# State weights turned on the matrix engine instead of the vector engine, and a shifted weight conversion, in an attention block that feeds a gated MLP

## The chip, the cores and the metric

The kernel runs on one core of a Trainium2 chip. A core has a matrix engine (TensorE, PE in the profile; its weight loads are PEld), a vector engine (VectorE, DVE), a scalar engine (ScalarE, ACT), GpSimd (POOL) and a sync engine (SP) that here only issues transfers. The engines run their own instruction streams in order and wait for each other by semaphores. The metric is device time in microseconds (us) of one execution; lower is better.

## The reference

Two blocks follow each other. The first is attention between 512 tokens and 32 state rows per head, in both directions; the second is an MLP over the 8 x (512 + 32) = 4352 rows that the first one makes, with the gate h·cos(h).

```python
B, H, S, Ns, D = 8, 8, 512, 32, 64           # d_model 512, d_ff 2048
scores  = x @ state.T / sqrt(D);  a  = softmax(scores);   xread = a @ state
scores2 = state @ x.T / sqrt(D);  a2 = softmax(scores2);  sread = a2 @ x
x2 = concat([xread, sread], axis=2)          # to (B*(S+Ns), H*D)
h = x2 @ w_in
out = (h * cos(h)) @ w_out
```

The weights arrive as 64-bit floats and are turned into 32-bit floats on the chip.

## The kernel before, in words

The order of all work is written out by hand. The loop at the end of the kernel goes through 144 tiles ("steps"): 16 for the tokens of each of the 8 batches (one tile is 128 of the 2048 hidden columns, for 512 tokens), and 16 for the state rows of all batches together. This text calls the 16 steps of batch b "loop b" and numbers them 0 to 15.

What one step does, in the order in which it is issued: `hidden` (L479) makes h in a PSUM bank, out of `aT` (the normalised attention weights of the batch) and `sw` (the product of state and w_in, so that xread is never formed); there are two such banks, so the h of a step waits for the last reader of h two steps before. `gate` (L485, ACT) rounds, `gate2` (L488, DVE) subtracts, `gate3` (L493, L494, ACT) takes Abs and Sin, `gate4` (L500, DVE) multiplies h by the cosine and writes the tile g. `output` (L544) multiplies g of the tile three steps back (four in loop 0) with w_out.

The output product takes pairs of batches and computes 7 block products instead of 8, in the manner of Strassen and Winograd: w_out lies in four blocks a11, a12, a21, a22; `blocks` (L858, POOL) makes the sums s1, s2, s4 and s3 of them once, s3 in the place of a21; `minus` (L506) makes differences of g. The two halves of the loops are phases: 0 and 1 in even loops, 2 and 3 in odd ones. Products that a pair leaves over (`p7` with s3, `p4` with a22) are done during the next pair, one in two of three steps, which is why steps differ in length. `keep_product` (L555 on ACT, L557 on DVE) and `plus` (L550) take finished products out of PSUM into `held`, `store` (L571) turns them on DVE and SP writes them out.

`plan(b)` says what else is issued at which step of loop b; this is the attention of batch b+1. `pe` is issued right after h, `x_act` and `x_dve` after gate2, `y_act` and `y_dve` after gate4:

- `tokens_turned` (L298, DVE): x of the batch, which SP loaded into `xT`, is transposed in 32x32 blocks. In batches 0 and 1 PE does it (L271) instead.
- `scores` (L316, PE) into the two PSUM banks `at`; `max1` (L330), `spread1` (L336), `shift` (L353), `max2` (L346), `exps` (L357 and L362, ACT, each between loads of the function table), `sums` (L330 again), `norm1` (L383), which leaves `aT`.
- The weights of the state's read, `z2` (in xT[:, 2:4]), have to be transposed into `a2T` (in xT[:, 0:2], where `spread` was). For batches 0 and 1 `turn` (L389) does it with 8 PE transposes and `turn_kept` (L394) copies the results from the banks `at` on ACT. For batches 2 to 7 `turn_block` (L404) does it in 16 DVE transposes of 32x256 elements.
- `reads` (L416, PE), in two halves; after the second one SP is given the loads of the next x (`load_tokens`, 16 transfers into xT, and `load_x`, 4 into x_b). `keep` (L426, DVE), `keep2` (L432, PE) and `keep3` (L437, ACT) finish the state's rows.
- `products` (L316, PE) make `sw` for 512 hidden columns, `products_kept` (L453, ACT) copies it out of PSUM; a quarter serves four steps.

The weight conversion is a chain of parts, `convert`: SP loads 1 MB of raw weights into unused g tiles, ACT makes two passes (parts 1 and 2; L224, L227), DVE three (a, b, c; L231, L233, L236), POOL adds (d; L241), and part f fetches the load three further on. `conv_at` gives the step of parts 1 and 2; the others follow one step later. All of it is in loop 0, with two more at the very end. Conversions 10 and 11 are the last of w_in, 12 and 13 are a12, 14 and 16 a22, 15 and 17 a21.

Of the kernel before, what the change touches and what calls it, by code (L numbers as in the profile page):

```python
# [12 lines left out]
ALU = mybir.AluOpType  # L13
# [10 lines left out]
def kernel(  # L24
# [8 lines left out]
    nc = tc.nc  # L33

    B, H, S, D = x.shape
    Ns = state.shape[2]
    Dm, Dff = moe_w_in.shape
    P = 128
    NK = Dm // P
# [32 lines left out]
    a11, a12 = w_out[:, 0, 0:NH], w_out[:, 0, NH:NF]  # L72
    a21, a22 = w_out[:, 1, 0:NH], w_out[:, 1, NH:NF]
# [174 lines left out]
    class Attention:  # L248
# [147 lines left out]

        def turn_block(self, k, q):
            src = self.z2.rearrange("p j (c q i) -> p q (j c) i", q=P // 32,  # L400
                                    i=32)
            dst = self.a2T.rearrange("p j c m -> p (j c) m")
            rows = slice(Ns * k, Ns * k + Ns)
            nc.vector.transpose(out=dst[32 * q:32 * q + 32, :, rows],  # L404
                                in_=src[rows, q])

        def reads(self, j):  # L410
            cols = slice(2 * D * j, 2 * D * j + 2 * D)
# [49 lines left out]
    def part(b, name, *args):  # L461

        if b not in attn:
            attn[b] = Attention(b)
        getattr(attn[b], name)(*args)
        if (name, args) == ("reads", (1,)) and b + 1 < B:
            if b > 0:
                attn[b + 1] = Attention(b + 1)
                attn[b + 1].load_tokens()
            load_x(b + 1)  # L470
# [21 lines left out]
    def gate3(t):  # L492
        nc.scalar.activation(t.q, t.q, func=ACTF.Abs)  # L493
        nc.scalar.activation(t.q, t.q, func=ACTF.Sin, bias=halfpi,  # L494
                             scale=-TWO_PI)
# [261 lines left out]
    def plan(b):  # L757
        pe, x_act, y_act, x_dve, y_dve = [
            {s: [] for s in range(NF)} for _ in range(5)]

        def prod(s, b, nt, *bank):
            pe[s].append((b, "products", nt) + bank)
            if b == 1 and nt > 0:
                x_dve[s].append((b, "products_taken", nt) + bank)
            else:
                x_act[s].append((b, "products_kept", nt) + bank)

        def pairs(s, b, name, kept, i):
            pe[s] += [(b, name, i), (b, name, i + 1)]
            x_act[s].append((b, kept, i))  # L770
            y_act[s].append((b, kept, i + 1))

        def early(b, s):
            if b == 1:
                pairs(s[0], b, "tokens", "tokens_kept", 0)
                pairs(s[1], b, "tokens", "tokens_kept", 2)
            else:
                for k in range(NK):
                    to = (x_dve, y_dve)[k % 2]
                    to[s[k // 2]].append((b, "tokens_turned", k))  # L780
            pe[s[2]].append((b, "scores"))
            x_dve[s[2]].append((b, "max1"))
            x_dve[s[3]].append((b, "spread1"))
            y_dve[s[3]].append((b, "shift"))
            x_dve[s[4]].append((b, "max2"))
            y_act[s[4]].append((b, "exps"))
            x_dve[s[5]].append((b, "sums"))
            y_dve[s[5]].append((b, "spread1"))
            x_dve[s[6]].append((b, "norm1"))

        def late(b, s):
            if b < 2:
                pairs(s[0], b, "turn", "turn_kept", 0)
            if s[1] is not None:
                pe[s[1]].append((b, "reads", 0))
            pe[s[2]].append((b, "reads", 1))
            x_dve[s[2]].append((b, "keep"))
            if len(s) > 3:
                turned(b, s[3])

        def blocks_turned(b, to):

            for i in range(16):
                to[i * 5 // 16].append((b, "turn_block", i % NK, i // NK))

        def turned(b, s):
            pe[s].append((b, "keep2"))
            x_act[s].append((b, "keep3"))


        if b == 0:
            pe[0].append((0, "products", 0, SIDE, HC, WC))
            y_dve[0] += [(0, "products_taken", 0, SIDE, HC, WC),
                         (0, "inverse2")]
            prod(7, 0, 2, SIDE)
            prod(11, 0, 3)
            prod(13, 1, 0, MAIN)
            late(0, (1, 2, 3, 4))
            early(1, (5, 6, 7, 8, 9, 10, 11))
            late(1, (12, 13, 14))  # L820
        else:


            odd = b % 2
            bank = (SIDE,) if b == 1 else ()
            if b == 1:
                turned(1, 0)
                prod(0, b, 1, MAIN)
            elif odd:
                prod(0, b, 1)  # L830
                turned(b, 1)
            else:
                late(b, (None, None, 0))
                prod(2, b, 1)
                turned(b, 3)
            prod(4, b, 2, *bank)
            prod(9 if odd else 10, b, 3, *bank)
            if b + 1 < B and odd:
                prod(13, b + 1, 0)
                early(b + 1, (2, 3, 5, 6, 7, 8, 9))  # L840
                blocks_turned(b + 1, (x_dve[12], y_dve[12], x_dve[13],
                                      y_dve[13], x_dve[14]))
                pe[15].append((b + 1, "reads", 0))
            elif b + 1 < B:
                early(b + 1, (4, 5, 6, 7, 8, 9, 10))
                blocks_turned(b + 1, (y_dve[10], x_dve[11], y_dve[11],
                                      x_dve[12], y_dve[12]))
                late(b + 1, (None, 13, 14))
                prod(15, b + 1, 0)
        return pe, x_act, y_act, x_dve, y_dve  # L850


    conv_at = {s: 4 + i for i, s in enumerate(
        (0, 1, 2, 3, 4, 5, 6, 7, 8, 10, 11, 12, 13, 14))}
    conv_at.update({B * NF + 5: N_LOADS, B * NF + 7: N_LOADS + 1})

    def blocks(op, out_, a, b, r):
        nc.gpsimd.tensor_tensor(out_[:, r], a[:, r], b[:, r], op=op)  # L858

    lo, hi = slice(0, NH // 2), slice(NH // 2, NH)  # L860
    block_at = {15: (ALU.add, s1, a21, a22, lo),
                17: (ALU.add, s1, a21, a22, hi),
                18: (ALU.subtract, s2, s1, a11, lo),
                19: (ALU.subtract, s2, s1, a11, hi),
                20: (ALU.subtract, s4, a12, s2, lo),
                21: (ALU.subtract, s4, a12, s2, hi),
                22: (ALU.subtract, s3, a11, a21, lo),
                23: (ALU.subtract, s3, a11, a21, hi)}
    LAG = 3

    line = []
# [1 line left out]
    for step, t in enumerate(all_tiles):  # L873
        s = step % NF
        if s == 0 and t.b < B:
            steps = plan(t.b)
        todo = [p[s] if t.b < B else [] for p in steps]

        def go(n):
            for p in todo[n]:  # L880
                part(*p)

        last, conv = conv_at.get(step - 1, -1), conv_at.get(step, -1)
        if step == B * NF + (0 if f64 else 8):
            fetch(N_LOADS + 2)
        if step == 4:
            warm(1, acc[MAIN][0])
        if step != 1:
            hidden(t)
        if step == 0:  # L890
            hidden(all_tiles[1])
            warm(3, acc[MAIN][0])
            gate(t)
            gate2(t)
            convert(3, "bcdf")
            convert(4, "1a")
            go(0)
        else:
            go(0)
            if step == 5:  # L900
                states(1, acc[SIDE][1])
            gate(t)
            gate2(t)
            if step == 3:
                warm(4, acc[MAIN][0])
                part(0, "products", 1, SIDE)
                part(0, "products_kept", 1, SIDE)
            go(1)
            go(3)
            if step == 1:  # L910
                convert(4, "bcdf")
            elif last >= 0:
                convert(last, "abcdf")
            if conv >= 0 and not todo[1]:
                convert(conv, "1")
        gate3(t)
        if later:
            later.pop(0)()
        gate4(t)
        if conv >= 0 and todo[1] and step > 0:  # L920
            convert(conv, "1")
        if t.pair is not None:
            sums(t)
        if step == 6:
            states_kept(1, acc[SIDE][1])
        go(2)
        if conv >= 0:
            convert(conv, "2")
        go(4)
        if step in block_at:  # L930
            blocks(*block_at[step])
        if t.pair is not None:
            sums2(t)
        while len(line) >= (LAG if step >= 2 * NH else LAG + 1):
            output(line.pop(0))
        line.append(t)
# [32 lines left out]
```

## Time and profile before

| | |
|---|---|
| median of 5 runs | 795.44 us (794.85 to 795.65) |
| profiled execution: time, span | 795.71 us, 793.9 us |
| granted PE clock | 0.997 of full speed |
| busy: PE, DVE, ACT, POOL | 766.5, 472.9, 383.0, 178.5 us |
| DVE: L404, 32x256 transposes | 96, 41.8 us |
| ACT: L394, copies of turned weights | 4, 2.3 us |
| POOL: L858, block sums | 8, 18.8 us |

Busy time counts instructions in flight; a matrix instruction's end is modelled, so that consecutive ones overlap by some tenths of a microsecond. The distance between starts tells more. In timeline lines the columns are start and length in us, engine, source line, operation, tiles (written <- read), array use, shape and number of instructions merged into the line; a bracket holds the engine's idle time just before and what ended it. In lines of waits they are who waited for whom, total us, number of times and the longest.

### The profile page before, as it was taken

Reading aid. Unit: us, or ns where it says so; the run is one execution under the profiler, and the core shown is the slowest. Engines: PE = TensorE matmul, PEld = TensorE weight load, DVE = VectorE, ACT = ScalarE, POOL = GpSimd, SP = SyncE. Lnnn points to the kernel's source line nnn. Section 1 sums busy time; section 2 is a strip of 40 time slices with the busy share of each in tenths; the row PEclk is TensorE's granted clock in tenths of the full one; section 3 lists DMA queues with packets and bytes.
Section 4 is the critical chain, followed back from the end, with each engine's and each line's share of the span. In section 5 each row is a group of like instructions: output and inputs, shape, how many; then the busy total and the mean of one; then the engine's idle time right before and its main releaser. Section 6 shows DMA issues by size and latency. Waiting matters only on the chain.

```text
span 793.9 us, 7552 instructions
## 1 busy us (share of the span) xinstructions
PE 766.5 (97%) x2616; PEld 336.9 (42%) x2616; DVE 472.9 (60%) x771; ACT 383.0 (48%) x614; POOL 178.5 (22%) x119
## 2 busy tenths in 40 slices
PE   8998899899999999999999999999999999999997
PEld 4443333344443444344344444344444444455554
DVE  5879887762468567773658467853566456432531
ACT  3877964642445445643464436433463445322222
POOL 2343358683000000451000000740000004610200
PEclk9999999999999999999999999999999999999999
DMA  8585371003210520105000710105100114000021
GB/s 238 159 229 195 114 152 28 0 1 61 45 26 1 97 49 14 27 4 103 14 13 5 129 27 3 25 14 93 27 0 1 26 28 101 31 1 13 14 40 40
DMA packets 161957, 43.48 MB, mean 55 GB/s; under 512 B 153920, under 2 KB 153920, under 8 KB 161920
## 3 DMA queue, kind: packets, MB, share of 16 engines
q1 hardware_dynamic: 161024, 42.49, 24.6%
q10 hardware_dynamic: 768, 0.39, 0.2%
q8 instruction: 20, 0.33, 0.2%
q0 software_dynamic: 128, 0.13, 0.1%
q14 instruction: 17, 0.14, 0.1%
HBM read 34.08 MB, written 8.91 MB: 54 GB/s over the span
## 4 chain that ended last, share of the span: by engine, by line
PE 69%; DVE 13%; ACT 13%; issue 2%; DMA 1%; POOL 1%; SPq 0%; DVEq 0%; POOLq 0%
PE o L544 37%; PE h L479 22%; PE at L316 4%; PE o L664 3%; DVE q L488 3%; ACT q L493 3%; ACT q L494 3%; DVE g_all L500 2%; DVE xT L404 2%; PE at L416 2%; ACT xT L362 1%; ACT q L485 1%; DVE xT L336 1%; ACT L494 1%; ACT aT L357 1%
## 5 line engine op out<-in xcount | busy, mean ns | idle before, releaser
L479 PE MATMUL h<-aT,sw 128*128 128x512 f32 x512 | 241.6, 594 | 15.0 <-DVE g_all L500 12.8
L544 PE MATMUL o<-g_all,w_out 128*128 128x512 f32 x512 | 236.9, 599 | 1.2 <-POOL w_out L241 1.2
L506 POOL TENSOR_TENSOR g_all<-g_all 128x512 f32<-128x512 f32 x80 | 112.0, 1420 | 454.3 <-DVE g_all L500 450.8
L485 ACT ACTIVATE q<-h 128x512 f32<-128x512 f32 (+1 forms) x144 | 82.1, 570 | 258.9 <-PE h L479 258.9
L488 DVE SCALAR_TENSOR_TENSOR q<-q,h 128x512 f32<-128x512 f32 (+1 forms) x144 | 94.1, 654 | 188.7 <-ACT q L485 188.2
L544 PE MATMUL o<-g_all,s 128*128 128x512 f32 x384 | 177.8, 598 | 0.5 <-DVE held L557 0.5
L500 DVE TENSOR_TENSOR g_all<-h,q 128x512 f32<-128x512 f32 (+1 forms) x144 | 94.9, 659 | 103.0 <-ACT q L494 99.4
L479 PEld LDWEIGHTS h<-aT,sw 128*128 128x128 f32 x512 | 96.3, 190 | 139.9 <-issue 111.6
L544 PEld LDWEIGHTS o<-g_all,w_out 128*128 128x128 f32 x512 | 93.9, 190 | 127.0 <-issue 120.4
L493 ACT ACTIVATE q<-q 128x512 f32<-128x512 f32 (+1 forms) x144 | 87.6, 609 | 110.9 <-DVE q L488 110.8
L544 PEld LDWEIGHTS o<-g_all,s 128*128 128x128 f32 x384 | 71.1, 190 | 94.9 <-issue 87.9
L494 ACT ACTIVATE q<-q,halfpi 128x512 f32<-128x512 f32 (+1 forms) x144 | 100.5, 698 | 4.5
L404 DVE STREAM_TRANSPOSE xT<-xT 32x256 f32<-32x256 f32 x96 | 41.8, 435 | 1.8
L241 POOL TENSOR_TENSOR w_out<-w_out,s 128x1024 int32<-128x1024 int32 x10 | 23.9, 2392 | 79.4 <-DVE w_out L236 79.4
L506 DVE TENSOR_TENSOR g_all<-g_all 128x512 f32<-128x512 f32 x48 | 33.2, 692 | 1.6
L453 ACT COPY sw<-at 128x512 f32<-128x512 f32 x50 | 26.8, 588 | 9.0 <-PE at L316 9.0
L479 PE MATMUL h<-sT,w_in 128*128 128x256 f32 x128 | 30.2, 379 | 0.0
L664 PE MATMUL o<-w_out,g_all 128*128 128x512 f32 x64 | 29.6, 592 | 0.0
L479 PEld LDWEIGHTS h<-sT,w_in 128*128 128x128 f32 x128 | 24.3, 190 | 10.1 <-issue 6.2
L316 PE MATMUL at<-w_in,stT 64*32 64x512 f32 x400 | 27.2, 601 | 0.0
L241 POOL TENSOR_TENSOR w_in<-w_in,s 128x1024 int32<-128x1024 int32 (+1 forms) x10 | 19.6, 1964 | 32.7 <-DVE w_in L236 18.6
L550 DVE SCALAR_TENSOR_TENSOR held<-o,held 128x512 f32<-128x512 f32 x40 | 25.4, 680 | 2.4 <-PE o L544 2.3
(84 smaller groups left out, 453.9 us busy)
## 6 DMA issues: line engine op xcount, KB each, us to landing
out_dram<-ot SPq DMA_DIRECT2D x132, 64.0 KB, 2.0
g_all<-in_moe_w_out_dram SPq DMA_DIRECT2D x8, 1024.0 KB, 5.2
g_all<-in_moe_w_in_dram SPq DMA_DIRECT2D x6, 1024.0 KB, 5.2
xT<-in_x_dram SPq DMA_DIRECT2D x96, 64.0 KB, 2.4
x_b<-in_x_dram SPq DMA_DIRECT2D x24, 256.0 KB, 4.7
x_b<-in_x_dram SPq DMA_DIRECT2D x16, 128.0 KB, 4.2
g_all<-in_moe_w_in_dram SPq DMA_DIRECT2D x4, 512.0 KB, 6.1
x_b<-in_moe_w_out_dram SPq DMA_DIRECT2D x1, 1024.0 KB, 6.2
```

Of the source, the lines that this page charges most:

```text
L241: nc.gpsimd.tensor_tensor(bits, bits, e.bitcast(I32), op=ALU.add)
L316: nc.tensor.matmul(out=(to or at)[j][Ns * k:Ns * k + Ns, 0:n], lhsT=w[D * j:D * j + D, self.b, Ns * k:Ns * k + Ns], rhs=r(slice(D * j, D * ...
L404: nc.vector.transpose(out=dst[32 * q:32 * q + 32, :, rows], in_=src[rows, q])
L479: nc.tensor.matmul(out=t.hp, lhsT=t.lhs(i), rhs=t.rhs(i), start=(i == 0), stop=(i == t.kn - 1))
L485: nc.scalar.activation(t.q, t.hp, func=ACTF.Copy, bias=MAGIC)
L488: nc.vector.scalar_tensor_tensor(out=t.q, in0=t.q, scalar=MAGIC, in1=t.hp, op0=ALU.subtract, op1=ALU.subtract)
L493: nc.scalar.activation(t.q, t.q, func=ACTF.Abs)
L494: nc.scalar.activation(t.q, t.q, func=ACTF.Sin, bias=halfpi, scale=-TWO_PI)
L500: nc.vector.tensor_tensor(t.g, t.hp, t.q, op=ALU.mult)
L506: engine.tensor_tensor(out, a, b, op=ALU.subtract)
L544: nc.tensor.matmul(out=acc[bank][ch], lhsT=w[:, i, P * ch:P * ch + P], rhs=g.g, start=(i == 0), stop=(i == NH - 1))
L664: nc.tensor.matmul(out=acc[MAIN][i], lhsT=t.g[:, P * i:P * i + P], rhs=w_out[:, :, t.f, :], start=(t.n_th == 0), stop=(t.n_th == NF - 1))
```

## The change

`turn_block` and its scheduling go; every batch uses `turn` on PE and `turn_kept` on ACT. Even and odd loops now have one plan: products at steps 0, 4, 9 and 14, token transposes at steps 1 and 2 (loop 1: 2 and 3, as before), scores at 5, exps at 7, norm1 at 9, turns at 10, reads at 11 and 12, keep2 at 15. Before, even loops had their products at steps 2, 4, 10 and 15, the token transposes at 4 and 5, scores at 6, exps at 8, norm1 at 10 and reads at 13 and 14, and the second reads of odd loops stood at step 0 of the following one.

In loop 0, conversions 10 to 17 are issued one step later than before (steps 6 and 9 of loop 0 now start none, before it was 9 alone), so the last ends in loop 1. The block sums s1, s2, s4 follow one step later, and s3 is made in loop 2 (steps 32 and 33 of the whole sequence) and not in loop 1 (22 and 23). In step 3 the copies of a product out of PSUM are issued after Abs and Sin of that step, not before them.

```diff
-        def turn_block(self, k, q):
-            src = self.z2.rearrange("p j (c q i) -> p q (j c) i", q=P // 32,
-                                    i=32)
-            dst = self.a2T.rearrange("p j c m -> p (j c) m")
-            rows = slice(Ns * k, Ns * k + Ns)
-            nc.vector.transpose(out=dst[32 * q:32 * q + 32, :, rows],
-                                in_=src[rows, q])
...
         def late(b, s):
-            if b < 2:
-                pairs(s[0], b, "turn", "turn_kept", 0)
-            if s[1] is not None:
-                pe[s[1]].append((b, "reads", 0))
+            pairs(s[0], b, "turn", "turn_kept", 0)
+            pe[s[1]].append((b, "reads", 0))
             pe[s[2]].append((b, "reads", 1))
...
         else:
-            odd = b % 2
             bank = (SIDE,) if b == 1 else ()
             if b == 1:
                 turned(1, 0)
-                prod(0, b, 1, MAIN)
-            elif odd:
-                prod(0, b, 1)
-                turned(b, 1)
-            else:
-                late(b, (None, None, 0))
-                prod(2, b, 1)
-                turned(b, 3)
+            prod(0, b, 1, *[MAIN for _ in bank])
             prod(4, b, 2, *bank)
-            prod(9 if odd else 10, b, 3, *bank)
-            if b + 1 < B and odd:
-                prod(13, b + 1, 0)
-                early(b + 1, (2, 3, 5, 6, 7, 8, 9))
-                blocks_turned(b + 1, (x_dve[12], y_dve[12], x_dve[13],
-                                      y_dve[13], x_dve[14]))
-                pe[15].append((b + 1, "reads", 0))
-            elif b + 1 < B:
-                early(b + 1, (4, 5, 6, 7, 8, 9, 10))
-                blocks_turned(b + 1, (y_dve[10], x_dve[11], y_dve[11],
-                                      x_dve[12], y_dve[12]))
-                late(b + 1, (None, 13, 14))
-                prod(15, b + 1, 0)
+            prod(9, b, 3, *bank)
+            if b + 1 < B:
+                prod(14, b + 1, 0)
+                early(b + 1, (1 + (b == 1), 2 + (b == 1), 5, 6, 7, 8, 9))
+                late(b + 1, (10, 11, 12, 15))
...
     conv_at = {s: 4 + i for i, s in enumerate(
-        (0, 1, 2, 3, 4, 5, 6, 7, 8, 10, 11, 12, 13, 14))}
+        (0, 1, 2, 3, 4, 5, 7, 8, 10, 11, 12, 13, 14, 15))}
...
-    block_at = {15: (ALU.add, s1, a21, a22, lo),
-                17: (ALU.add, s1, a21, a22, hi),
-                18: (ALU.subtract, s2, s1, a11, lo),
-                19: (ALU.subtract, s2, s1, a11, hi),
-                20: (ALU.subtract, s4, a12, s2, lo),
-                21: (ALU.subtract, s4, a12, s2, hi),
-                22: (ALU.subtract, s3, a11, a21, lo),
-                23: (ALU.subtract, s3, a11, a21, hi)}
+    block_at = {16: (ALU.add, s1, a21, a22, lo),
+                18: (ALU.add, s1, a21, a22, hi),
+                19: (ALU.subtract, s2, s1, a11, lo),
+                20: (ALU.subtract, s2, s1, a11, hi),
+                21: (ALU.subtract, s4, a12, s2, lo),
+                22: (ALU.subtract, s4, a12, s2, hi),
+                32: (ALU.subtract, s3, a11, a21, lo),
+                33: (ALU.subtract, s3, a11, a21, hi)}
...
                 part(0, "products", 1, SIDE)
-                part(0, "products_kept", 1, SIDE)
             go(1)
...
         gate3(t)
+        if step == 3:
+            part(0, "products_kept", 1, SIDE)
         if later:
```

More of the change, by code (lines that the diff above doesn't have):

```diff
@@ L799, in late @@
                 turned(b, s[3])
-        def blocks_turned(b, to):
-            for i in range(16):
-                to[i * 5 // 16].append((b, "turn_block", i % NK, i // NK))
         def turned(b, s):
```

## The prediction

> **What bounds the kernel now.** I read the page's engine shares first, then the matrix engine's (PE's) waits, then PE's timeline tile by tile. A *step* is one tile: PE's group at L479, named h, followed by what is issued until the next h. "Loop b" is the 16 steps 0 to 15 of batch b; its loop also prepares batch b+1.
>
> ```profile
> PE 766.5 (97%) x2616; PEld 336.9 (42%) x2616; DVE 472.9 (60%) x771; ACT 383.0 (48%) x614; POOL 178.5 (22%) x119
> ```
>
> PE is the bound: 27 us of 793.9 are not busy, so an engine taken off the vector engine (DVE) gains only where PE waits for it.
>
> ```profile
> PE h L479 <- DVE g_all L500: 12.8, 9, 2.7
> PE h L479 <- ACT sw L453: 2.2, 2, 1.7
> PE at L416 <- DVE xT L404: 0.6, 3, 0.2
> PE o L544 <- DVE held L557: 0.5, 2, 0.2
> ```
>
> Of the 12.8 us, 3.1 lie after 160 us; most waits are in loop 0, where weights are converted, and in loop 1. But a modelled matmul end hides part of a wait, so I go by start times. A quad (four 128x512 matmuls) takes 1.72 us from start to start (387.31 to 389.03 below), a 16-matmul group at L316 or L416 1.22 with its change-over (6.37 us for a step that holds one and three quads, 5.15 without). Any surplus is a stall. Loop 4 (even), PE:
>
> ```profile
> 387.31 1.88 PE L479 MATMUL h<-aT,sw 128*128 128x512 f32 x4
> 389.03 1.88 PE L544 MATMUL o<-g_all,w_out 128*128 128x512 f32 x4
> 390.75 1.88 PE L479 MATMUL h<-aT,sw 128*128 128x512 f32 x4
> 392.56 2.00 PE L316 MATMUL at<-xT,stT 64*32 64x512 f32 x16
> 394.48 1.98 PE L544 MATMUL o<-g_all,w_out 128*128 128x512 f32 x4
> ...
> 430.39 0.43 PE L416 MATMUL at<-x_b,xT 128*64 128x128 f32 x2
> 431.01 1.09 PE L416 MATMUL at<-x_b,xT 128*64 128x128 f32 x14 [0.19 <-DVE xT L404]
> ```
>
> The scores at 392.56 start on three quarters of their input: the last token transpose (L298) runs on DVE from 392.67. Step 6 takes 7.27 us where 6.37 is its work: 0.90 lost. Step 13 takes 5.28 against 4.65: 0.63 lost to the last L404. Step 11 takes 5.31 against 5.15: 0.17. Loops 2 and 6 show the same to 0.02. Loop 3 (odd), PE:
>
> ```profile
> 325.55 1.88 PE L544 MATMUL o<-g_all,s 128*128 128x512 f32 x4
> 329.00 1.98 PE L479 MATMUL h<-aT,sw 128*128 128x512 f32 x4 [1.57 <-DVE g_all L500]
> 330.82 2.74 PE L544 MATMUL o<-g_all,s 128*128 128x512 f32 x6
> 333.79 1.13 PE L544 MATMUL o<-g_all,s 128*128 128x512 f32 x2 [0.23 <-DVE held L557]
> ```
>
> Step 10 is 5.17 us for two quads (3.43): 1.74 lost, behind exps (step 7), sums and norm1 on DVE. Step 11 is 5.75 for 5.15: 0.60 lost at L557. Loop 5 repeats it; loop 1 loses 2.13 and 0.10 there.
>
> **The change part by part.** The profiled execution took 795.71 us around its span of 793.9, 0.27 above the median of 795.44; I take the same difference off the median.
>
> *Turns on PE.* Removed: 96 DVE transposes at L404, 0.436 us each, 41.8 us in six batches. Added: 8 PE transposes per batch and two ScalarE (ACT) copies of 0.574 (L394). Their price is in loop 0, which does them already:
>
> ```profile
> 51.19 1.04 PE L271 MATMUL at<-ident,x_b 128*128 128x128 f32 x8
> 52.06 0.60 PE L142 MATMUL o<-ident,s 128*128 128x128 f32 x4
> ...
> 89.64 1.04 PE L389 MATMUL at<-ident,xT 128*128 128x128 f32 x8
> 90.51 1.88 PE L544 MATMUL o<-g_all,w_out 128*128 128x512 f32 x4
> ```
>
> Eight take 0.87 us start to start, both times. In loops 2, 4, 6 step 10 has no stall: 3 x 0.87 = +2.6. In loops 1, 3, 5 they fall between 325.55 and 329.00, into the 1.74 (or 2.13) stall: 0, or +2.6 if that cover goes. The copies: the first waits for norm1 (it overwrites `spread`), which ends at 327.7, and fits into ACT's idle 2.37 us before 330.30; the second delays ACT's L555 from 331.60 to 332.2, before PE needs that bank (332.5). Behind it, the next L485 slips 0.5, and DVE's L488 at 333.66 hides that: 0. Bounds 0 to 12 x 0.574 = +6.9, taken 0 because ACT is idle by 1 to 3 us in these steps.
>
> [...]
>
> *Even loops, stalls removed.* The token transposes move to steps 1 and 2, the scores to step 5: 0.90 goes. No L404 holds the reads or L557: 0.63 and 0.17 go. 3 x 1.70 = -5.1. Next late would be what stalls odd loops: exps now in step 7, norm1 in 9. Here PE reaches the h of step 11 by two quads and the turns later (1.72 + 1.72 + 0.87 = 4.3), DVE has three L506 of 0.69 less; 4.3 + 2.1 - 1.74 leaves 4.7 us of slack. Bounds: -5.1 to 0.
>
> *Odd loops.* The first reads now stand in step 11 between h and the quads that wait for L557; their 1.22, moved from step 15, cover the 0.60: -1.2 in loops 3 and 5, -0.1 in loop 1. Bounds -1.3 to 0. The stall of step 10 stays: its chain is the same.
>
> *Other moves.* Second reads with keep (DVE, 4 x 0.295) go to step 12, where DVE has lost 2.7 us of L404; keep2 and keep3 to step 15; products from 2, 10, 13 or 15 to 0, 9, 14: same instructions, same PE time, 0. With the second reads go 16 xT and 4 x_b loads on SP: they block it 12.4 us for xT (from 432.13) and land 2.4 later, about 3 steps; they are needed 5 steps on (about 26 us). Stores queue behind them as now; the next, three steps later, waits at most 1 to 2 us, for nobody. 0; if a load came late, one step of 5 us.
>
> *Loop 0.* PE, DVE and ACT take turns here. (a) Step 3: the two sw copies wait for PE until 43.64, with Abs and Sin behind them; now these run in ACT's 3.08 us of idleness before. The product on DVE (47.07, after 1.99 idle) can follow at 45.1. PE gains nothing until step 5 (it waits for POOL's w_out until 47.65); from then ACT is about 1.4 ahead and PE's 0.51 wait at 57.05 goes. (b) Step 7 loses its conversion (0.65 + 0.69 + 1.22 on DVE). DVE's L488 of step 8, at 69.64, now follows h, two conversion parts and ACT's L485: 67.9, 1.74 earlier. (c) Steps 8 to 11 hold as many conversions as before; the chain of waits is ACT and DVE throughout, so 1.74 remains. (d) The conversion at step 11, though, is now the first half of a12, which before was done at step 9:
>
> ```profile
> 90.74 1.22 DVE L236 SCALAR_TENSOR_TENSOR w_out<-g_all,w_out 128x1024 int32<-128x1024 int32 x1
> ...
> 92.11 2.36 POOL L241 TENSOR_TENSOR w_out<-w_out,s 128x1024 int32<-128x1024 int32 x1 [9.05 <-DVE w_out L236]
> ```
>
> POOL's add ends at 94.47 - 1.74 = 92.7; the first product with a12 (step 12, 90.51 before) would be ready at 88.8 and waits 3.9 us. From there PE's own work to the h of loop 1 is 1.82 + 14.03 (92.62 to 106.65, unstalled): 108.6, against 108.41, whose 1.76 stall is used up. +0.2. Lower end -0.5 (DVE's product, 107.9, then bounds); upper end +1.9 (no 1.74). (e) The last conversion is now in step 16, ahead of that step's product: it ends at 117.9, and h needs it at 118.6. POOL's first half of s1 ends at 123.2, needed at 123.8. 0; one more POOL op of 2.37 if not.
>
> *s3.* Two POOL ops of 2.36 leave steps 22 and 23, where nobody waited, for 32 and 33; p7 reads them three steps later. 0.
>
> **Sum:** +2.6 - 5.1 - 1.3 + 0.2 = -3.6, so 795.44 - 3.6 = 791.8 us.
>
> **Rivals.** (A) The late a12 keeps PE waiting and no head start reaches it: +1.7 on the sum, 793.5. For: two handovers between ACT and DVE decide it. Against: freed DVE time is in the rows. (B) The turns show in odd loops too, because the stall shrinks with DVE's relief: +2.6, 794.4. Against: no L404 stood before step 10. (C) Slower than before: exps one step earlier in even loops, ahead of the short step 8, put the odd loops' stall there. Each pays 1.74 + 0.60, hiding its 0.87: 3 x 1.47 = +4.4 on the sum, 796.2, and past 797.0 from another 0.3 us a loop. It decides once more than the 4.7 us of slack is used. Against: nothing in the rows uses it. (D) Better: the a12 wait is shorter and DVE bounds, or odd stalls shrink with turns hidden: -4.3 to -5.5, 791 to 790.
>
> **How the numbers follow.** Forecast 0.53, A 0.15, B 0.10, C 0.12, D 0.10. Own range of the forecast 790.9 to 792.8. The range 790.3 to 794.6 leaves out C and part of D. 0.2% (1.6 us) is about what a measurement can tell: faster, below 793.85, holds the forecast, D and two thirds of A, 0.73; same the rest of A, B and a third of C, 0.19; slower, above 797.03, two thirds of C, 0.08.
>
> **What would show it.** Right: steps 6 and 13 of even loops free of surplus, step 10 of 6.0 us there; step 10 of odd loops unchanged near 5.2 with eight transposes in it; a POOL wait of 3 to 4 us before step 12's product in loop 0, and loop 1's first h near 108.6. Wrong: a DVE wait at h in even loops, h of loop 1 past 110, or PE waiting for xT loads at the scores.

## The result, and the profile after

| | before | after |
|---|---|---|
| median | 795.42 us (43 executions) | 793.92 us (23 executions), 0.9981 of before, 95% interval 0.9975 to 0.9986 |
| profiled execution: time, span | 795.71, 793.9 | 793.92, 792.1 |
| granted PE clock, mean | 0.997 | 0.994 |
| busy: PE, DVE, ACT | 766.5, 472.9, 383.0 | 769.8, 430.3, 390.0 |

The change made the kernel 1.5 us faster; 3.6 were forecast. The time is inside the range, and 0.07 us above the line (793.85) that I had drawn between faster and no change.

The page's engine shares of the kernel after, and the granted clock over 40 slices of the span (in tenths, 9 is 90% or more):

```profile
PE 769.8 (97%) x2664; PEld 341.9 (43%) x2664; DVE 430.3 (54%) x675; ACT 390.0 (49%) x626; POOL 178.7 (23%) x119
...
PEclk9999899999999999999999999999999999999999
```

DVE lost 42.6 us of work, and PE's 48 more instructions are the transposes. The 8 in the fifth slice (79 to 99 us, in loop 0) is new (before, all 40 are 9); it is where the forecast failed.

PE's waits, kernel after:

```profile
PE h L469 <- DVE g_all L490: 7.9, 7, 2.7
PE o L534 <- POOL w_out L241: 5.0, 2, 3.8
...
PE h L469 <- ACT sw L443: 0.5, 1, 0.5
```

PE's wait for DVE at h fell from 12.8 to 7.9 us, that for ACT's `sw` from 2.2 to 0.5 (why is told under `a12_early`), and no wait for turned weights or for `held` is left among the first ones. The wait for POOL's w_out grew from 1.2 to 5.0. In the kernel before it was:

```profile
PE o L544 <- POOL w_out L241: 1.2, 1, 1.2
```

I compare where each loop stands, by the start of h counted from the first h of the execution (loops 2 and later at their step 4, because the plans put different work into the first ones):

| work | forecast | measured, after minus before |
|---|---|---|
| loop 0 (to the first h of loop 1) | +0.2 | +1.59 |
| loop 1 | -0.1 | +0.08 |
| loops 2, 4, 6 | -0.83 each | -0.83, -0.81, -0.81 |
| loops 3, 5 | -0.60 each | -0.48, -0.49 |
| loop 7 and the state's tiles | 0 | 0.00 |
| sum | -3.6 | -1.75 |

The profile's sum of -1.75 agrees with the -1.8 of the two spans and lies in the interval of the medians (-2.0 to -1.1).

**Even loops.** Loop 4 after, PE's timeline:

```profile
387.54 1.88 PE L469 MATMUL h<-aT,sw 128*128 128x512 f32 x4
389.35 1.09 PE L316 MATMUL at<-xT,stT 64*32 64x512 f32 x16
390.37 1.98 PE L534 MATMUL o<-g_all,w_out 128*128 128x512 f32 x4
392.19 1.88 PE L469 MATMUL h<-aT,sw 128*128 128x512 f32 x4
393.91 3.60 PE L534 MATMUL o<-g_all,w_out 128*128 128x512 f32 x8
397.34 1.88 PE L469 MATMUL h<-aT,sw 128*128 128x512 f32 x4
...
412.29 1.88 PE L469 MATMUL h<-aT,sw 128*128 128x512 f32 x4
414.01 1.04 PE L389 MATMUL at<-ident,xT 128*128 128x128 f32 x8
414.88 3.60 PE L534 MATMUL o<-g_all,w_out 128*128 128x512 f32 x8
418.32 1.88 PE L469 MATMUL h<-aT,sw 128*128 128x512 f32 x4
420.13 1.09 PE L406 MATMUL at<-x_b,xT 128*64 128x128 f32 x16
...
431.06 1.88 PE L469 MATMUL h<-aT,sw 128*128 128x512 f32 x4
432.78 1.88 PE L534 MATMUL o<-g_all,w_out 128*128 128x512 f32 x4
434.49 1.02 PE L469 MATMUL h<-aT,sw 128*128 128x512 f32 x2
```

No line has a bracket: PE never waits in them (the last line is cut off where the view ends). The scores, now in step 5 (387.54 to 392.19, 4.65 us), have no surplus, nor has step 6 (5.15, it was 7.27 with the scores in it) or step 13 (431.06 to 434.49, 3.43). Step 10 is 6.03 us, and the eight transposes in it take 0.87 (414.01 to 414.88).

**Odd loops.** Loop 3 after, PE's timeline:

```profile
324.55 1.88 PE L469 MATMUL h<-aT,sw 128*128 128x512 f32 x4
326.27 1.04 PE L389 MATMUL at<-ident,xT 128*128 128x128 f32 x8
327.14 1.88 PE L534 MATMUL o<-g_all,s 128*128 128x512 f32 x4
329.73 1.98 PE L469 MATMUL h<-aT,sw 128*128 128x512 f32 x4 [0.71 <-DVE g_all L490]
331.65 1.09 PE L406 MATMUL at<-x_b,xT 128*64 128x128 f32 x16
332.67 3.70 PE L534 MATMUL o<-g_all,s 128*128 128x512 f32 x8
336.21 1.88 PE L469 MATMUL h<-aT,sw 128*128 128x512 f32 x4
```

Step 10 is 5.18 us with eight transposes in it (5.17 before, without): the bracket at h fell from 1.57 to 0.71, and the stall hides them. Step 11 is 6.48, not 6.37: its h, which begins as a wait ends, takes 1.92 to the next start, against 1.81 in step 11 of loop 4.

**Loop 0.** PE's timeline after, steps 12 and 13, and then three stretches of it (columns: stretch, its length, busy time and instructions of PE, PEld, DVE, ACT and POOL, the granted clock, DMA share, GB/s):

```profile
85.91 1.98 PE L469 MATMUL h<-aT,sw 128*128 128x512 f32 x4
87.73 1.04 PE L389 MATMUL at<-ident,xT 128*128 128x128 f32 x8
92.59 3.26 PE L534 MATMUL o<-g_all,w_out 128*128 128x512 f32 x4 [3.82 <-POOL w_out L241]
95.64 2.34 PE L469 MATMUL h<-aT,sw 128*128 128x512 f32 x4
```

```profile
92.50:93.40 0.90, 0.81 (x2) 0.57 (x3) 0.87 (x2) 0.87 (x2) 0.03 (x1) 0.86 1.06 400
93.40:96.60 3.20, 3.20 (x5) 1.14 (x5) 2.24 (x3) 2.40 (x3) 1.38 (x1) 0.51 0.49 144
96.60:99.00 2.40, 2.40 (x22) 0.56 (x22) 0.35 (x1) 0.60 (x1) 0.97 (x1) 1.00 0.89 331
```

The forecast had the wait for POOL's add of a12 (3.9 forecast, 3.82 measured) and the start of the product (92.7 forecast, 92.59 measured). What it lacked comes after the wait: from 93.4 to 96.6 only five matmuls fit into 3.2 us, and the granted clock is 0.51. The quad at L534 takes 3.05 us to the next start rather than 1.72. From the product to the first h of loop 1 it takes 17.28 us (92.59 to 109.87) where I had summed 15.85.

### The profile page after: what moved, and what is told of

Read it like the earlier page. It is cut to its first block, busy times and chain, and to the rows that moved or that the text cites. A ratio compares the mean times of both kernels' runs of the same rounds, so it can differ in the third digit from the quotient of the medians.

```text
span 792.1 us, 7554 instructions
## 1 busy us (share of the span) xinstructions
PE 769.8 (97%) x2664; PEld 341.9 (43%) x2664; DVE 430.3 (54%) x675; ACT 390.0 (49%) x626; POOL 178.7 (23%) x119
## 4 chain that ended last, share of the span: by engine, by line
PE 83%; DVE 7%; ACT 6%; issue 1%; POOL 1%; DMA 1%; SPq 0%; DVEq 0%; POOLq 0%
PE o L534 45%; PE h L469 27%; PE at L316 4%; PE o L654 3%; PE at L406 2%; DVE q L478 1%; DVE g_all L490 1%; DVE xT L336 1%; ACT q L483 1%; ACT xT L362 1%; DVE aT L383 1%; ACT q L475 1%; ACT q L484 1%; PE o L316 1%; ACT aT L357 1%
## 5 line engine op out<-in xcount | busy, mean ns | idle before, releaser
L534 PE MATMUL o<-g_all,w_out 128*128 128x512 f32 x512 | 237.8, 601 | 5.0 <-POOL w_out L241 5.0
L534 PE MATMUL o<-g_all,s 128*128 128x512 f32 x384 | 177.4, 598 | 0.0
L534 PEld LDWEIGHTS o<-g_all,w_out 128*128 128x128 f32 x512 | 94.2, 190 | 129.9 <-issue 119.2
L534 PEld LDWEIGHTS o<-g_all,s 128*128 128x128 f32 x384 | 70.8, 190 | 91.9 <-issue 87.9
L561 DVE STREAM_TRANSPOSE ot<-held 128x512 f32<-128x512 f32 x32 | 22.2, 692 | 0.0
```

Source lines behind the costliest of these rows:

```text
L534: nc.tensor.matmul(out=acc[bank][ch], lhsT=w[:, i, P * ch:P * ch + P], rhs=g.g, start=(i == 0), stop=(i == NH - 1))
```

## The experiments

Two theories for those five slow matmuls: (1) the granted clock was halved because PE had idled, or (2) the traffic at that moment (DVE, POOL and transfers all busy around the late conversion). The second question was which part of the change gives and which takes.

**PE kept busy during the wait.** Matmuls on a tile of zeros into a free PSUM bank, four (`fill4`) or two (`fill2`), issued in step 12 ahead of the output product; the rest is the kernel after. Each of these matmuls stands in the trace as two instructions of 0.43 us, so four are `x8` at L711.

```diff
             sums2(t)
+        if step == 12:
+            warm(4, acc[SIDE][1])
         while len(line) >= (LAG if step >= 2 * NH else LAG + 1):
```

> The changed kernel with four filler matmul pairs (8 x 0.43 us, into the free SIDE bank) ahead of step 12's first a12 product in loop 0, where PE idles 3.82 us and then runs five matmuls at 0.85 us. Theory 1 (the idle stretch lets the clock gate halve PE's clock for 3.4 us, and those five matmuls lose 1.45 us on the path): product still starts near 92.6, granted clock 1.00 after it, h of loop 1 near 108.4, about 792.5 against 793.9. Theory 2 (the slow matmuls come from traffic of POOL, DVE or DMA at that moment): unchanged, 793.9.

> As fill4 with two filler pairs, so that about 2.1 us of idle time stay in one piece before the product. Theory 1 with a limit that lies between 2.1 and 2.7 us of idleness (a 2.68 us gap at 76.6 us is followed by a half clock too): no half clock, about 792.5. If a gap of 2.1 us is enough to halve it: 793.9. Theory 2: 793.9.

Measured: four, 791.50 us, 0.9950 of before (0.9938 to 0.9963); two, 791.52 us, 0.9953 (0.9940 to 0.9965). PE's timeline and one stretch with four:

```profile
87.67 1.04 PE L389 MATMUL at<-ident,xT 128*128 128x128 f32 x8
88.54 3.60 PE L711 MATMUL o<-g_all 128*128 128x512 f32 x8
92.54 1.99 PE L534 MATMUL o<-g_all,w_out 128*128 128x512 f32 x4 [0.40 <-POOL w_out L241]
94.36 1.88 PE L469 MATMUL h<-aT,sw 128*128 128x512 f32 x4
```

```profile
93.40:96.60 3.20, 3.20 (x15) 1.13 (x21) 2.20 (x3) 2.71 (x4) 1.43 (x1) 1.00 0.46 134
```

The product starts at the same time as in the kernel after (92.54 and 92.59) and with the same transfers beside it (144 and 134 GB/s, DVE 2.24 and 2.20 us), but at full clock: the quad takes 1.82 us, and the first h of loop 1 comes 1.66 us earlier (85.50 us after the first h of the execution, not 87.16). By the medians, work that computes nothing gained 2.4 us (1.7 by the two profiles). Theory 1 holds, theory 2 falls. With four, loop 0 is also close to what the prediction had: 15.58 us from the product to loop 1, where 15.85 were summed, and the state's tiles start 3.44 us earlier than before, where 3.6 were forecast. Both medians lie a microsecond below the 792.5 expected under theory 1; that is not explained.

With two the profiled execution still had the slow stretch, after an idle time of 2.09 us, which the expectation had held to be too short:

```profile
87.96 1.88 PE L711 MATMUL o<-g_all 128*128 128x512 f32 x4
91.94 3.29 PE L534 MATMUL o<-g_all,w_out 128*128 128x512 f32 x4 [2.09 <-POOL w_out L241]
```

```profile
92.50:96.20 3.70, 3.70 (x6) 1.49 (x5) 2.49 (x3) 2.65 (x4) 1.64 (x1) 0.54 0.53 167
```

That execution took 792.78 us; the other four took 791.32 to 791.57 and their mean clocks were 0.999 or 1.000, against 0.996. So, by the mean clocks, the same program either meets the drop or not. More on this in the last section.

**One part at a time.** The one plan for all loops with the turns on PE, and nothing else of the change, in the kernel before (`plan_only`); everything else of the change alone (`shift_only`); the eviction of step 3 alone (`evict_only`); and the kernel after with the conversions and the sums s1, s2, s4 back at their steps (`conv_back`).

The core of plan_only, against before:

```diff
-            odd = b % 2
...
-                prod(13, b + 1, 0)
-                early(b + 1, (2, 3, 5, 6, 7, 8, 9))
-                blocks_turned(b + 1, (x_dve[12], y_dve[12], x_dve[13],
-                                      y_dve[13], x_dve[14]))
...
+                early(b + 1, (1 + (b == 1), 2 + (b == 1), 5, 6, 7, 8, 9))
+                late(b + 1, (10, 11, 12, 15))
```

Of shift_only, against before:

```diff
-        (0, 1, 2, 3, 4, 5, 6, 7, 8, 10, 11, 12, 13, 14))}
+        (0, 1, 2, 3, 4, 5, 7, 8, 10, 11, 12, 13, 14, 15))}
...
+                32: (ALU.subtract, s3, a11, a21, lo),
+                33: (ALU.subtract, s3, a11, a21, hi)}
```

Of both shift_only and evict_only, against before:

```diff
-                part(0, "products_kept", 1, SIDE)
...
         gate3(t)
+        if step == 3:
+            part(0, "products_kept", 1, SIDE)
```

Of conv_back, against after:

```diff
-        (0, 1, 2, 3, 4, 5, 7, 8, 10, 11, 12, 13, 14, 15))}
+        (0, 1, 2, 3, 4, 5, 6, 7, 8, 10, 11, 12, 13, 14))}
...
-    block_at = {16: (ALU.add, s1, a21, a22, lo),
+    block_at = {15: (ALU.add, s1, a21, a22, lo),
...
```

> The kernel before with the turns on PE and the one plan for all loops alone: conversions, all block sums and the step 3 eviction as before. My theory: the even loops gain 0.82 us each and loops 3 and 5 0.48 each, 3.4 in all; 792.0 against 795.4. Rival (PE transposes cost more on the chip than the rows say, the gain came from elsewhere): 794 or more.

> The kernel before with the other half of the change alone: conversions and block sums one step later, s3 in loop 2, step 3 eviction next to Sin; vector-engine transposes and old plans stay. My theory: loop 0 is the changed kernel's, slower than before by 1.5 us, 796.9 against 795.4. Rival (the shift helps by itself): 794 or less.

> The kernel before with one part of the change: the eviction of step 3 placed behind that step's gates. My reading: step 8 starts 1.4 us earlier and, with the conversions and the transposes' plan as before, nothing later takes it back: about 793.9 beside 795.3 before (0.998). Rival: the head start is only worth something together with the later conversions or the other plan; without them the waits on VectorE's gate products at the end of loop 0 swallow it: 795.3 (1.000), h of loop 1 where it was.

> The changed kernel with conversions 10 to 17 and the sums s1, s2, s4 at the steps of the kernel before; turns on PE, s3 in loop 2 and the step 3 eviction stay. My theory (the shift costs 1.5 us net, because a12 comes late): no POOL wait at step 12, the old DVE waits of loop 0 back, about 792.0 to 791.2, faster than the changed kernel. Rival (the shift pays for itself and the turns cost more than I read): 793.9 or more.

| | median | ratio to before (95%) | first h of loop 1, us after the first h | start of the state's tiles against before, by the profile |
|---|---|---|---|---|
| before | | | 85.57 | 0 |
| after | 793.92 | 0.9981 (0.9975 to 0.9986) | 87.16 | -1.75 |
| plan_only | 791.65 | 0.9957 (0.9944 to 0.9969) | 85.56 | -3.45 |
| shift_only | 797.84 | 1.0036 (1.0023 to 1.0050) | 87.18 | +1.69 |
| evict_only | 793.77 | 0.9984 (0.9976 to 0.9993) | 84.10 | -1.47 |
| conv_back | 790.68 | 0.9939 (0.9927 to 0.9952) | 84.12 | -4.87 |

By the profiles the parts add up: -3.45 for the plan and +1.69 for the rest make -1.76, and after measured -1.75. The eviction gives 1.47 of its own and keeps it through loop 1; the later conversions then take 3.1 back (from 84.1 to 87.16): 1.66 by the clock, as the filled wait showed, and the other 1.4 by the wait itself (85.50 with the wait filled, 84.12 without it). The plan and the eviction came as expected, conv_back half a microsecond better (791.2 to 792.0 expected). The shift alone was expected at +1.5: its profile shows +1.7, but its median is +2.9 (95% interval +1.8 to +4.0). That difference is not explained; the profiled execution was the fastest of the five (797.06), and the others have no profile.

No run has the one plan with the turns left on DVE, so the 3.45 us of plan_only are not divided between the two. By the rows of before, 0.80 of the 1.70 us that each even loop loses stood behind L404, and the turns on PE cost 0.87 there; the other 0.90 stood behind the token transposes, which the plan moved.

PE's waits of shift_only show the same wait for POOL as in after:

```profile
PE o L544 <- POOL w_out L241: 5.0, 2, 3.8
```

**Only a12 early.** The kernel after with the first conversion of a12 one step earlier (step 9), so that it is in time for step 12.

```diff
-        (0, 1, 2, 3, 4, 5, 7, 8, 10, 11, 12, 13, 14, 15))}
+        (0, 1, 2, 3, 4, 5, 7, 8, 9, 11, 12, 13, 14, 15))}
```

> The changed kernel with conversion 12 (first half of a12) started in step 9, so converted in step 10, which has none; the rest stays. My theory (only a12's place keeps the 1.74 us head start of loop 0 from PE): the wait at step 12 and the half clock go, DVE bounds loop 0 again, loop 1 starts at about 107, 791.0 to 791.5. Rival (DVE is full in step 10, behind exps, sums and spread): the chain slips by 1.5 us or more there and the time stays near 793.

Measured 792.62 us, 0.9962 (0.9948 to 0.9976): 1.3 us below after, with intervals that just touch, and over a microsecond worse than expected. The wait for POOL at step 12 is gone, and the first h of loop 1 stands at 85.80. In the profiled execution three other waits for DVE, of 2.68, 2.45 and 1.86 us, are each followed by a half clock: the h behind them takes 3.78, 2.90 and 3.29 us, where it takes 1.9 to 2.0 at a clock of 1. (It was the slowest of the five, 793.87 us at a mean clock of 0.991; the others had 0.995 to 0.997.) The first is the 2.68 us that every kernel here has before the h of step 11; this time the clock stayed low through two windows (6.8 us):

```profile
74.70:78.10 3.40, 1.30 (x4) 0.23 (x2) 3.30 (x6) 3.34 (x4) 0.00 (x0) 0.99 0.42 164
78.10:81.50 3.40, 2.82 (x4) 1.18 (x4) 1.32 (x3) 2.65 (x7) 2.36 (x1) 0.50 0.61 190
81.50:84.90 3.40, 3.40 (x19) 0.73 (x18) 3.26 (x7) 3.37 (x5) 0.00 (x0) 0.50 0.31 118
```

Step 11 took 7.82 us (6.61 after). In after one slow window stood there as well (a clock of 0.50 from 79.5 to 82.9 us), without a price, since PE would have waited 1.7 us for ACT's `sw` at the next h (1.69 before, gone after). My expectation had priced the wait that goes, and again not the clock. The time is nearer to the rival's (near 793), but steps 9 and 10 take 4.17 and 6.38 us as in after, so no slip from a full DVE shows in them.

**The turns' price.** The eight transposes issued twice (the second time over the same result), in loops 3 and 5 (`turn2_odd`) or in loops 2, 4 and 6 (`turn2_even`, where the condition is `b % 2 == 0`), else the kernel after.

```diff
                 early(b + 1, (1 + (b == 1), 2 + (b == 1), 5, 6, 7, 8, 9))
+                if b % 2 == 1 and b > 1:
+                    pe[10] += [(b + 1, "turn", 0), (b + 1, "turn", 1)]
                 late(b + 1, (10, 11, 12, 15))
```

> The changed kernel with the eight PE transposes issued twice in loops 3 and 5 (the second time over the same result). My theory (step 10 of odd loops idles, so that PE work is free there): 0.87 us of added work meets 0.71 us of idle time left, +0.2 each, 794.2. Rival (the turns are paid in odd loops too): +0.87 each, 795.6.

> The changed kernel with the eight PE transposes issued twice in loops 2, 4 and 6. My theory (no idle time there, eight cost 0.87 us): +2.6, 796.5. [...] If DVE's chain still bounds step 10 there: 0.

Measured: odd, 793.47 us, 0.9979 (0.9969 to 0.9989), no different from after, so the +0.2 a loop that was expected does not show; even, 795.91 us, 1.0014 (1.0005 to 1.0023), and by the profile 2.62 us more over the three loops (the spans, 795.6 and 792.1, differ by 3.5; the other 0.87 came from a window at half clock at the first h of that execution), where 2.6 was expected. Step 10 of loop 3, then of loop 4:

```profile
323.77 1.88 PE L469 MATMUL h<-aT,sw 128*128 128x512 f32 x4
325.49 1.91 PE L389 MATMUL at<-ident,xT 128*128 128x128 f32 x16
327.23 1.88 PE L534 MATMUL o<-g_all,s 128*128 128x512 f32 x4
328.95 1.98 PE L469 MATMUL h<-aT,sw 128*128 128x512 f32 x4
```

```profile
414.08 1.88 PE L469 MATMUL h<-aT,sw 128*128 128x512 f32 x4
415.80 1.91 PE L389 MATMUL at<-ident,xT 128*128 128x128 f32 x16
417.55 3.60 PE L534 MATMUL o<-g_all,w_out 128*128 128x512 f32 x8
420.98 1.88 PE L469 MATMUL h<-aT,sw 128*128 128x512 f32 x4
```

In loop 3 sixteen transposes fill the stall to the last tenth, and step 10 is still 5.18 us; in loop 4 it grows from 6.03 to 6.90. So the turns cost 0 in one kind of loop and 0.87 in the other, as the prediction had them.

**Only the last conversions late.** The kernel after with the conversions due at steps 6 to 12 of loop 0 where they were before, and the last ones, with the second half of s1 and the other sums, one step later (`tail_late`), beside conv_back once more.

```diff
-        (0, 1, 2, 3, 4, 5, 7, 8, 10, 11, 12, 13, 14, 15))}
+        (0, 1, 2, 3, 4, 5, 6, 7, 8, 10, 11, 12, 14, 15))}
...
-    block_at = {16: (ALU.add, s1, a21, a22, lo),
+    block_at = {15: (ALU.add, s1, a21, a22, lo),
```

> The kernel after with the conversions due at steps 10 to 15 where they were before, and the last ones one step later (conversions 16 and 17 and the last block sums). My reading: the conversion for step 12 is in time, PE does not idle there and its clock stays whole, and the wait of 1.8 us on VectorE that the kernel with all conversions back has at the start of loop 1 shrinks: 789.2 to 790.7, 0.992 to 0.994 of before. Rival: the last conversions, later, make PE wait there as in the kernel after, or a half-clock stretch follows: 791 to 792.5.

> The kernel with all conversions back where they were, once more beside the one with only the last ones later: 790.7, as the first time.

Both take 790.14 us: 0.9931 (0.9920 to 0.9943) and 0.9939 (0.9927 to 0.9951). By the profile the wait of 1.8 us at the start of loop 1 is gone in the one,

```profile
105.10 1.88 PE L469 MATMUL h<-aT,sw 128*128 128x512 f32 x4
...
116.10 1.98 PE L469 MATMUL h<-aT,sw 128*128 128x512 f32 x4 [0.92 <-DVE g_all L490]
```

and half of it comes back two steps later as 0.92, which leaves 0.8 us; the medians do not tell that from nothing. Either of the two is faster than before (by 4.9 us) and than after (0.9981, so by 3.3 and 4.0 us): the change without its later conversions, in tail_late those of 10 to 15 (w_in, a12, half of a22 and half of a21), in conv_back all.

## Why the prediction was right or wrong

- *Turns on PE, +2.6, bounds to +6.9.* Right, in even and odd loops (2.62 for a second set in the even ones, nothing in the odd ones); the copies on ACT cost nothing that shows.
- *Even loops, -5.1.* Right: -0.81 to -0.83 net per loop, -0.83 forecast. No DVE wait at h took their place, so rival C's mechanism is refuted; odd loops kept their cover, which refutes rival B.
- *Odd loops, -1.3.* The mechanism held, the size was off by 0.12 in each of loops 3 and 5: I counted step 11 as if its h had not begun at the end of a wait, which costs 0.1 in its first matmul. Loop 1 is 0.18 off, by two waits of 0.1 in its steps 2 and 3.
- *Loop 0, (a) and (b).* Right in sum (step 12's h 1.77 earlier, 1.74 forecast), wrong in parts. The eviction of step 3, which I let gain 0.5, gave 1.47: the steps 6 and 7 are each 0.73 shorter. The step without a conversion, for which I had claimed all of 1.74, gave 0.3.
- *Loop 0, (d): the step that failed.* "From there PE's own work to the h of loop 1 is 1.82 + 14.03" assumed that PE works after a wait as before it. It was 17.28 us and not 15.85, because the 3.82 us of idleness cost another 1.66 of clock; with the wait filled (`fill4`) it was 15.58. Of the 1.85 us between forecast and profile 1.4 are this term; 0.4 are the tenths in the odd loops and loop 1. The upper end of +1.9 stood there for a lost head start, not for this, so that the time still fell into the range was luck.
- *Loop 0, (e), s3 and the loads on SP.* Put at nothing, and all but 0.1 is: in the kernel after the first half of s1 ends on POOL at 124.96 and the product that reads it starts at 125.02, which is the 0.1 us in step 3 of loop 1. Loop 7 and the state's tiles are even, and loop 0's eviction alone (1.47) gives as much as eviction and s3 together (1.42, conv_back less plan_only).

Rival A's time, 793.5, is close to what came, but for another reason: the head start did reach step 12. Nothing in my sum or in the rivals let a wait touch the clock. In the trace of before the clock stood at 1 behind PE's longest wait in loop 0, 2.67 us before the h of step 11. It did hold a warning elsewhere: a half clock from 7.8 to 11.2 us, behind two shorter waits (last section).

## What to carry to other kernels

When a change makes the matrix engine wait, price the wait and then the half clock behind it: here up to 1.7 us (1.66 in after, by `fill4`) after idle times of 2.09 us (`fill2`) and 3.82 us (after), and nothing where PE would have waited again anyway (step 11 of after, 2.68 us). Here a new wait of 3.8 us in one place took back 3.1 of the 4.9 us that the rest of the change gains, so list the longest waits and those that lie close together, not only the sum over the kernel. If the wait can't go, matmuls on zeros can fill it: here four of them gained 2.4 us by the medians and 1.7 by the profiles.

## What the runs showed of the hardware

In the clock records of the profiles the granted clock only has the values 1 and 0.5. In before it is 0.5 from 7.79 to 11.20 us of the span (and again in the last microsecond), in after from 7.82 to 11.23, from 79.50 to 82.91 and from 93.15 to 96.56. Each of these four drops lasts 3.413 us, and the stretches at 1 between them are whole multiples of that (in after 68.267 and 10.240 us, 20 and 3 times). I call one part of this grid of 3.413 us a window. It stands differently against the program from one execution to another: a drop begins at 79.5 us in after, at 78.1 in a12_early and at 80.1 in conv_back. A drop lasted one window, in one case two (a12_early, 0.50 from 78.1 to 84.9 us). Laying PE's idle times over this grid, in the 13 profiles of this case (those of before, after and the eleven experiments), from 23 us on, where no window holds more than one long wait:

| idle time inside one window | next window at half clock |
|---|---|
| 2.03 to 3.09 us | 15 of 15 |
| 1.85 to 1.96 us | 2 of 9 |
| 0.9 to 1.79 us | 0 of 47 |

So in these profiles, from 23 us on, each wait with 2.03 us or more inside one window was followed by a half clock, and none with 1.79 or less was. A wait of 2.67 us left the clock at 1.00 in the kernel before (81 to 87 us), where the grid cut it into 0.93 and 1.74, but one of 2.68 us halved it in after (0.50 from 79.5 to 82.9 us), where all of it lay in one window. Of the wait of 3.82 us in after, 0.96 lay in one window and 2.85 in the next, and behind it the clock was 0.50 from 93.15 to 96.56 us.

Before 23 us PE has several short waits in one window. Six windows with 1.73 to 2.02 us of idle time in sum, and no single wait over 1.59, were each followed by a half clock, and four with 1.43 to 1.69 were not. One of the six is in the kernel before, with waits of 1.14 and 1.02 us for transfers of x:

```profile
4.40:7.70 3.30, 1.54 (x9) 0.92 (x8) 0.58 (x1) 0.58 (x1) 0.00 (x0) 1.00 1.26 226
7.80:11.20 3.40, 3.07 (x18) 2.67 (x24) 0.97 (x3) 1.27 (x3) 0.00 (x0) 0.50 1.05 353
```

The second of these waits begins at 7.08, so only 0.71 of it lies in the first window.

Still open: why idle times of 1.73 to 1.96 us fall on either side, why the clock stayed low for a second window in a12_early, where PE was idle for 0.58 us of the first and saw no wait in the second, and the 1.2 us by which (2.9 against 1.7) the median of shift_only exceeds its profile.
